# Gated linear attention and an MLP mixer on one core: block 5 by DMA transpose, batch 0 mixed into its transposed form, channel weights in three-chunk pieces, and another order

## The chip, the cores and the metric

One core of one Trainium2 chip runs the whole program in one launch. The metric is the device time in microseconds, a median of three runs. Inputs and the output lie in device memory as float32; matrix products run in bfloat16 with float32 sums in PSUM. The core has five instruction streams: PE (TensorE, matrix products), DVE (VectorE), ACT (ScalarE), POOL (GpSimd) and SP (SyncE, which here only issues transfers). The transfers themselves run on sixteen DMA engines that all queues share.

## The reference, cut to what matters

```python
B, H, S, D = 4, 8, 768, 48                      # batch, heads, time, head size
for t in range(S):                              # gated linear attention
    state = alpha[:, :, t, :, None] * state + k[:, :, t, :, None] * v[:, :, t, None, :]
    y[:, :, t] = einsum('bhd,bhde->bhe', q[:, :, t], state)
x = y as (B, S, H * D)                          # (4, 768, 384)
h  = relu(x.T @ w_tok1) @ w_tok2                # over time: 768 -> 256 -> 768
u  = x + h.T
h2 = relu(u @ w_ch1) @ w_ch2                    # over channels: 384 -> 1536 -> 384
out = u + h2
```

## The kernel before

**Blocks.** Time is cut into three blocks of 256 steps for each batch, so there are twelve attention blocks, 0 to 11 (block n belongs to batch n // 3). A block loads alpha, k, q and v (`ld_at`, `ld_kt`, `ld_qt`, `ld_vt`, 384 KB each, in runs of 384 bytes). Logarithms, a cumulative sum on PE (`cum`) and exponentials (`E`, `IE`) give the decay factors. Keys and queries are multiplied with them (`kk`, `qq`), transposed, multiplied with each other on PE (`G0`, `G1`), masked on DVE (`mask0`, `mask1`, a 128x1024 product each) and multiplied with v (`y0`, `y1`), together with what the carried state gives (`ia`, `ib`). `K`, `s`, `sa` and `sm` make the state. `x0` and `x1` take the two halves of the result out of PSUM. A block thus gives two of the six 128-row tiles x of its batch.

**How keys and queries are transposed.** In the blocks of KX and QX (6 to 11) by a DMA transpose that SP issues (`dk`, `dq`), and the query is then put in its final order by a copy (`pq`). In blocks 0 to 5 by eight PE transposes each (`trk`, `trq`) and a copy out of PSUM (`evk`, `evq`).

**Mixers.** For each batch: `t1` (12 products, 128x384) and `ht` (relu) give the hidden tokens, `t2` (12 products) and `u` (six adds of PSUM and x on DVE) give u with time on the partitions. u is then transposed into ut: in batch 0 (UP) on PE (`up`, 18 transposes of 128x128) with three copies `ut`; in batches 1 to 3 by two DMA transposes `ux_b_0`, `ux_b_1`, one for each half of u. `c1_b_mc_half` (three products; 24 of them in a batch) and `rt` (relu, ACT or DVE) give the hidden channels, `c2_b_i_q` (three products; 24 of them) and `o` (PSUM plus u, DVE) the output rows, which `st` stores.

**Weights.** Sixteen pieces of 384 KB (`ldw_`) are cast to bfloat16 by `cw_`. A piece of w_ch1 (`wc1`) is 128 of its 384 rows by 768 columns, so that a `c1` needs three pieces; a piece of w_tok2 (`wt2`) is 128 rows by 768 columns, and a `t2` needs both.

**What sets the order.** Nothing is scheduled at run time. The string ORDER names every operation with the engine that runs it (t PE, s ACT, v DVE, g POOL, y SP), and each engine does its operations in that order; BUFS gives the buffers. An operation at the head of its engine's list that waits holds up everything behind it there. `fN_` ahead of an operation are fillers: N products of 128x512 on zeros, which keep PE running (three of them are issued as one float32 product). SP's list holds all loads, all DMA transposes and some of the stores. Loads share 19 buffers of one class (`in`), so a load also waits until the former content of its buffer has been used.

Of the kernel before, what the change touches and what calls it, by code (L numbers as in the profile page):

```python
# [34 lines left out]
def dve(n, two=False):  # L35
    return {"DVE": (64 + n / (1.92 if two else 0.96), 157 + n / (1.92 if two else 0.96))}
# [61 lines left out]
KX = (6, 7, 8, 9, 10, 11)  # L98
QX = (6, 7, 8, 9, 10, 11)
KFN = 0  # L100
LAST = (3, 0)
UP = (0,)
# [18 lines left out]
def build(g):  # L121
# [8 lines left out]
    def fillers():  # L130
        for o in list(P.ops):
            nm = o.name
            if "PE" in o.eng and (nm[:4] in ("t1_0", "t2_0", "up_0") or nm.split("_")[-1][-1] in "0123" and nm[:2] not in ("t1", "t2", "up", "c1", "c2") and not nm.endswith("10") and not nm.endswith("11")):
# [182 lines left out]
    def mixer(b):  # L316
# [27 lines left out]
        uts = []
        if b in UP:
            for p in range(3):
                bank = V("one")
                o = P.op(f"up_{b}_{p}", pe([128] * 6), m0 + (3900 + 340 * p) * sc, writes=[bank],
                         reads=list(dict.fromkeys([us[2 * p][0], us[2 * p + 1][0]])),
                         preds=[us[2 * p][1], us[2 * p + 1][1]],  # L350
                         emit=lambda e, p=p, bank=bank: g.utr(bank, [us[2 * p][0], us[2 * p + 1][0]], p))
                uts.append(P.op(f"ut_{b}_{p}", either(dve(768, True), act(768)), m0 + (3950 + 340 * p) * sc, writes=[ut],
                                reads=[bank], preds=[o], emit=lambda e, p=p, bank=bank: g.utev(e, ut, bank, p)))
        else:
            for half in range(2):
                uts.append(P.op(f"ux_{b}_{half}", {"SP": (1240.0, 1240.0)}, m0 + (3900 + 500 * half) * sc, writes=[ut],
                                reads=[us[3 * half][0]], preds=[us[3 * half + i][1] for i in range(3)],
                                emit=lambda e, half=half: g.uxbar(ut, us[3 * half][0], half),
                                dma=("x", 1450.0, 1180.0, 480.0)))
        rts = []  # L360
        for mc in range(NDC):
            rt = V("rt")
            ro = []
            for half in range(2):
                bank = V("one")
                o = P.op(f"c1_{b}_{mc}_{half}", pe([384] * 3), m0 + (4900 + 975 * mc + 487 * half) * sc, writes=[bank],
                         reads=[ut], preds=(uts[0:2 + half] if b in UP else [uts[half]]) + [wl[("wc1", p)] for p in ((0, 1, 2) if mc < 6 else (3, 4, 5))],
# [5 lines left out]
        for i in range(NS):  # L373
            hold = 4000.0 if (i >= NS - 3 and b < B - 1) else 0.0
            cuts = [(0, HD // 2), (HD // 2, HD)] if (b, i) == LAST else [(0, HD)]
            for ci, (ca, cz) in enumerate(cuts):
# [3 lines left out]
                for q4 in range(4):  # L380
                    pp = []
                    for mc in range(3 * q4, 3 * q4 + 3):
# [6 lines left out]
                          reads=[bank, us[i][0]], preds=[prev],  # L389
# [576 lines left out]
```

## Time and profile before

| | us |
|---|---|
| median of 3 runs (162.3 to 162.38) | 162.38 |
| span of the profiled execution, first to last instruction | 160.5 |
| around the span, taking the profiled execution to have run like the median | 1.9 |
| PE busy | 154.6 |
| DVE, ACT, POOL busy | 114.9, 97.8, 80.8 |
| first product of mixer 0's `c1` | at 31.76 |
| first product of mixer 1's, 2's, 3's `c1` | at 67.80, 100.91, 133.81 |

The page of the profile has the busy time of each engine, then the span in 40 slices of 4.0 us with a digit (tenths) for each engine and for the DMA engines, and the groups of instructions by line of the source. The time line gives starts and durations, merged where one line runs several times in a row ("x12"). The DMA share of a stretch can come out above 1, so it is read against other stretches of the same trace. Times of a row are microseconds from the span's start; "mean ns" is the duration of one instruction. Matmuls follow each other faster than their duration, since they are pipelined.

### The profile page before, as it was taken

The page shows a single profiled execution, that of the slowest core. Times are in us where ns is not written, and L with a number is a line of the kernel's source. Part 1 is how long each engine was busy: PE and PEld are TensorE (multiplying, and loading weights), DVE is VectorE, ACT ScalarE, POOL GpSimd, SP SyncE. Part 2 cuts the span into 40 slices and gives each one's busy share as a digit, 9 for nine tenths or more (in the row PEclk, how much of TensorE's full clock was granted, in tenths as well). Part 3 has the DMA queues.
Part 4 walks back from the last instruction along what each step waited for, and adds up shares of the span by engine and source line. Part 5 has one row for each costly group of instructions (what it writes and reads, how often), then busy time and mean ns, then how long its engine had stood idle before and what let it go on. Part 6 is the DMA issues. An engine that isn't in the chain of part 4 may idle for free.

```text
span 160.5 us, 3971 instructions
## 1 busy us (share of the span) xinstructions
PE 154.6 (96%) x1563; PEld 97.1 (60%) x1563; DVE 114.9 (72%) x206; ACT 97.8 (61%) x179; POOL 80.8 (50%) x94
## 2 busy tenths in 40 slices
PE   7999989999999999999999999999999999999992
PEld 2545565766667676666667666566567665665661
DVE  6099994979889787989969758795886762464222
ACT  3789999998899955897563583269832203343000
POOL 5205897695973649389778852699523000000000
PEclk9999999999999999999999999999999999999999
DMA  4999999999999999999989999989701235111133
GB/s 122 320 324 317 317 374 311 339 333 306 316 347 324 275 278 272 210 228 319 241 202 298 239 315 204 217 196 134 196 21 62 87 79 169 49 49 53 49 129 116
DMA packets 76130, 35.05 MB, mean 218 GB/s; under 512 B 70352, under 2 KB 74320, under 8 KB 76112
## 3 DMA queue, kind: packets, MB, share of 16 engines
q1 hardware_dynamic: 73808, 31.76, 74.1%
q10 hardware_dynamic: 2304, 3.05, 5.3%
q8 instruction: 12, 0.20, 0.5%
q14 instruction: 6, 0.05, 0.1%
HBM read 25.17 MB, written 4.72 MB: 186 GB/s over the span
## 4 chain that ended last, share of the span: by engine, by line
PE 61%; DMA 12%; DVE 6%; ACT 6%; SPq 6%; POOL 4%; issue 3%; DVEq 0%; POOLq 0%
PE ps L907 22%; PE ps L902 21%; PE ps L643 11%; DMA in<-in_v_dram 6%; SPq L584 6%; DMA out_dram<-o 4%; PE ps L878 3%; PE ps L883 2%; DMA ut<-u 2%; DVE pkk L700 2%; DVE gtm L770 1%; PE ps L712 1%; DVE rt L875 1%; POOL vb L746 1%; POOL pkq L700 1%
## 5 line engine op out<-in xcount | busy, mean ns | idle before, releaser
L907 PE MATMUL ps<-wc,rt 128*128 128x384 bf16 (+1 forms) x300 | 52.4, 319 | 0.0
L902 PE MATMUL ps<-ut,wc 128*128 128x384 bf16 x288 | 50.3, 326 | 0.1
L902 PEld LDWEIGHTS <-wc 128*128 128x128 bf16 x288 | 27.1, 98 | 17.9 <-DMA ut<-u 0.6
L907 PEld LDWEIGHTS <-rt 128*128 128x128 bf16 x300 | 27.8, 98 | 16.0
L873 ACT ACTIVATE rt<-ps 128x384 bf16<-128x384 f32 x47 | 21.4, 492 | 23.6 <-PE ps L902 23.3
L875 DVE TENSOR_SCALAR rt<-ps 128x384 bf16<-128x384 f32 x49 | 25.6, 551 | 9.1 <-PE ps L902 8.9
L770 DVE TENSOR_TENSOR gtm<-ps,mk 128x1024 bf16<-128x1024 f32 x24 | 28.5, 1218 | 3.1 <-PE ps L643 2.8
L911 DVE TENSOR_TENSOR o<-ps,u 128x384 f32<-128x384 f32 (+1 forms) x25 | 13.2, 536 | 12.6 <-PE ps L907 10.1
L700 POOL TENSOR_TENSOR pkk<-in,IE 128x768 bf16<-128x768 f32 x8 | 14.5, 1817 | 3.3 <-DVE ss L844 2.3
L745 ACT CAST x<-ps 128x384 bf16<-128x384 f32 x20 | 9.2, 479 | 11.1 <-PE ps L643 9.5
L887 DVE TENSOR_TENSOR u<-ps,x 128x384 bf16<-128x384 f32 x24 | 12.0, 550 | 3.1 <-PE ps L883 2.5
L746 POOL CAST vb<-in 64x384 bf16<-64x384 f32 (+1 forms) x14 | 8.3, 594 | 10.4 <-DMA in<-in_v_dram 4.7
L692 POOL TENSOR_TENSOR in<-in,in 128x384 f32<-128x384 f32 x8 | 8.0, 1000 | 10.5 <-DVE u L887 3.8
L643 PE MATMUL ps<-rt 128*128 128x512 bf16 (+1 forms) x29 | 12.1, 515 | 1.1 <-DVE rt L541 1.1
L745 ACT CAST vb<-in 64x384 bf16<-64x384 f32 (+1 forms) x18 | 11.4, 634 | 0.8 <-DMA in<-in_v_dram 0.3
L700 POOL TENSOR_TENSOR pkq<-in,E 128x768 bf16<-128x768 f32 x6 | 10.9, 1818 | 0.6 <-DMA tpk<-pkq 0.3
L878 PE MATMUL ps<-x,wt 128*128 128x384 bf16 x48 | 11.0, 325 | 0.0
L844 POOL TENSOR_TENSOR ss<-tmp,E 128x384 bf16<-128x384 f32 x10 | 8.3, 833 | 4.2 <-DVE in L628 3.9
L841 DVE TENSOR_TENSOR tmp<-ps,ss 128x384 f32<-128x384 f32 x16 | 8.8, 552 | 1.8 <-PE ps L643 0.6
L883 PE MATMUL ps<-ht,wt 128*128 128x384 bf16 x48 | 9.1, 326 | 0.0
L643 PE MATMUL ps<-vb,gtm 128*128 128x48 bf16 x192 | 8.2, 183 | 0.2 <-DVE gtm L770 0.2
L643 PE MATMUL ps<-tpq,tpk 48*64 48x128 bf16 (+1 forms) x288 | 7.9, 218 | 0.4 <-POOL tpq L746 0.3
(94 smaller groups left out, 207.6 us busy)
## 6 DMA issues: line engine op xcount, KB each, us to landing
in<-in_alpha_dram SPq DMA_DIRECT2D x12, 384.0 KB, 5.1
in<-in_v_dram SPq DMA_DIRECT2D x12, 384.0 KB, 5.6
in<-in_k_dram SPq DMA_DIRECT2D x12, 384.0 KB, 5.2
in<-in_q_dram SPq DMA_DIRECT2D x12, 384.0 KB, 5.5
in<-in_moe_w_ch_dram SPq DMA_DIRECT2D x12, 384.0 KB, 5.9
out_dram<-o ACTq DMA_DIRECT2D x15, 192.0 KB, 1.8
in<-in_moe_w_tok_dram SPq DMA_DIRECT2D x4, 384.0 KB, 6.0
out_dram<-o SPq DMA_DIRECT2D x8, 192.0 KB, 2.2
```

The costliest lines, as they stand in the source:

```text
L643: return self.pe.matmul(out, lhsT=lhsT, rhs=rhs, start=start, stop=stop, skip_group_check=True)
L700: self.shared(self.eng[e].tensor_tensor(self.t(dst)[:, :, h0:h1, 0:D], self.t(src)[:, h0:h1].rearrange("p h s d -> p s h d"), bass.AP(tens ...
L745: return self.act.copy(d, s)
L770: self.nc.vector.tensor_tensor(self.t(gtm)[:, hf, :, :], self.pair(gp).rearrange("p a (j t) -> p (a j) t", t=128), bass.AP(tensor=m.tensor ...
L873: self.act.activation(d, s, AF.Relu)
L875: self.nc.vector.tensor_scalar_max(d, s, 0.0)
L878: self.pe.matmul(self.bank(bank)[:, 0:HD], lhsT=self.wt1[:, kc, m * 128 : m * 128 + 128], rhs=self.t(x), start=(kc == 0), stop=(kc == NS - 1))
L883: self.pe.matmul(self.bank(bank)[:, 0:HD], lhsT=self.wt2[:, kc, i * 128 : i * 128 + 128], rhs=self.t(hts[kc]), start=(kc == 0), stop=(kc = ...
L887: self.nc.vector.tensor_tensor(self.t(u)[:, i % 3], self.bank(bank)[:, 0:HD], self.t(x), ALU.add)
L902: self.pe.matmul(self.bank(bank)[:, 0:HD], lhsT=self.wc1[:, kc, mc * 128 : mc * 128 + 128], rhs=self.t(ut)[:, 3 * half : 3 * half + 3, kc, ...
L907: self.pe.matmul(self.bank(bank)[:, 0 : cz - ca], lhsT=self.t(rts[mc][0])[:, i * 128 : i * 128 + 128], rhs=self.wc2[:, mc, ca:cz], start=( ...
L911: self.nc.vector.tensor_tensor(self.t(o)[:, ca:cz], self.bank(bank)[:, 0 : cz - ca], self.t(u)[:, i % 3, ca:cz], ALU.add)
```

## The change

Four things, and then one list in place of another.

1. KX and QX begin with 5: block 5's `trk`, `trq`, `evk` and `evq` go, and `dk5`, `dq5` (DMA transposes issued by SP) and `pq5` (a copy, on POOL) come.
2. Batch 0 (UDIR) makes u directly in its transposed form. `xa_0_half_j` (three products of 128x128 with the identity) puts the transposed x into a PSUM bank, `tt_0_half_j` (two products of 128x384) adds the transposed token mix to it, and one copy `ut_0_half_j` takes the bank out as ut. The outputs still need u with time on the partitions, so two DMA transposes `un_0_0` and `un_0_1` make it from ut, and the adds `o_0_i` wait for them. `t2_0`, `u_0` and `up_0` are gone.
3. A piece of `wc1` is now 256 columns of all three row chunks (runs of 1 KB instead of 3 KB), and a `c1` needs one piece. A piece of `wt2` is 384 columns of both row chunks, and a `t2` or `tt` needs one.
4. ORDER and BUFS are other lists.

```diff
-KX = (6, 7, 8, 9, 10, 11)
-QX = (6, 7, 8, 9, 10, 11)
+KX = (5, 6, 7, 8, 9, 10, 11)
+QX = (5, 6, 7, 8, 9, 10, 11)
-UP = (0,)
+UP = ()
+UDIR = (0,)
...
+                    xa = P.op(f"xa_{b}_{half}_{j}", pe([128] * 3), ...
+                    o = P.op(f"tt_{b}_{half}_{j}", pe([384] * 2), ...
+                             reads=[h for h, _ in hts], preds=[h for _, h in hts] + [xa, wl[("wt2", half)]],
+                    evs.append(P.op(f"ut_{b}_{half}_{j}", either(act(384), dve(384)), ...
+                un = P.op(f"un_{b}_{half}", {"SP": (1240.0, 1240.0)}, m0 + 6000 * sc, writes=[u], reads=[ut], preds=evs,
...
-                         ... [wl[("wc1", p)] for p in ((0, 1, 2) if mc < 6 else (3, 4, 5))],
+                         ... [wl[("wc1", mc // 2)]],
...
-                          reads=[bank, us[i][0]], preds=[prev],
+                          reads=[bank, us[i][0]], preds=[prev, us[i][1]],
...
-            self.gated(dma(t, self.w[2][128 * c : 128 * c + 128, 768 * h : 768 * h + 768]), op)
+            self.gated(dma(t.rearrange("p (c m) -> p c m", c=3), w[:, :, 256 * piece : 256 * piece + 256]), op)
...
+    def xadd(self, bank, xs, j):
+        for i, x in enumerate(xs):
+            self.mm(self.bank(bank)[:, i * 128 : i * 128 + 128], self.t(x)[:, j * 128 : j * 128 + 128], self.idn, i == 0, False)
+
+    def tok2t(self, bank, half, j, hts):
+        for kc in range(NDT):
+            self.mm(self.bank(bank)[:, 0:HD], self.t(hts[kc])[:, j * 128 : j * 128 + 128],
+                    self.wt2[:, half, kc, :], False, kc == NDT - 1)
+
+    def utev3(self, e, ut, bank, half, j):
+        self.copy(e, self.t(ut)[:, 3 * half : 3 * half + 3, j, :], self.bank(bank)[:, 0:HD].rearrange("p (i t) -> p i t", i=3))
+
+    def unat(self, u, ut, half):
+        self.nc.sync.dma_start_transpose(self.t(u).rearrange("p i (j c) -> p (i j) c", j=NM),
+                                         self.t(ut)[:, 3 * half : 3 * half + 3].rearrange("p i j t -> p (i j t)"))
```

Parts of the lists that the prediction speaks of, sorted by engine from the two ORDER strings.

SP's list of before, up to the transposes of mixer 1's u:

```
at1 at0 vt0 kt0 qt0 kt1 vt1 at2 qt1 kt2 qt2 vt2 wt10 at3 wt11 wt21 wt20 at4 kt3 wc14 wc13 wc15 qt3 wc11 wc10 wc12 vt3
at5 qt4 kt4 wc21 wc20 wc22 kt5 wc23 qt5 vt4 wc24 wc25 at6 at7 vt5 kt7 at8 kt6 qt6 qt7 kt8 vt6 dk6 ux_1_0 st_0_0 dq6 ux_1_1
```

SP's list of after, up to the same point:

```
at0 at1 kt0 qt0 vt0 kt1 at2 qt1 vt1 kt2 qt2 at3 vt2 wt10 wt11 qt3 kt3 wt21 wt20 wc11 wc10 wc13 at4 wc14 vt3 wc12 qt4 wc15
at5 kt4 wc21 kt5 wc20 wc22 qt5 wc23 vt4 wc24 vt5 dk5 wc25 dq5 un_0_0 at6 at8 kt6 un_0_1 at7 kt8 qt6 vt6 qt7 ux_1_0 kt7 ux_1_1
```

Further parts of after's lists:

```
DVE: ... qq2 mask1_1 sa1_1 mask0_1 mask0_2 x1_1 sa0_2 mask1_2 q0r3 k0a3 qq3 ht_0_1 evq3 ut_0_1_1 ...
DVE: ... o_0_2 o_0_1 mask1_5 mask0_5 x1_5 k0a6 o_0_3 ht_1_0 u_1_1 u_1_2 u_1_0 u_1_4 o_0_4 u_1_3 u_1_5 ...
PE:  ... xa_0_1_0 xa_0_1_1 trq3 tt_0_1_0 xa_0_1_2 tt_0_1_2 tt_0_1_1 tt_0_0_1 trk3 tt_0_0_0 tt_0_0_2 c1_0_1_1 ...
PE:  ... c2_0_4_3 cum6 t2_1_1 t2_1_0 t2_1_2 t2_1_4 c2_0_0_3 t2_1_3 t2_1_5 c2_0_5_0 c2_0_5_1 c2_0_5_2 cum8 c2_0_5_3
     cum7 c1_1_1_0 ...
```

Fillers: 36 units in before (8+1, 8+1, 1, 1, 2, 4, 3, 2, 1, 1, 3), 24 in after (8+1, 2, 4+1, 3, 3, 2).

More of the change, by code (lines that the diff above doesn't have):

```diff
@@ L132, in fillers @@
             nm = o.name
-            if "PE" in o.eng and (nm[:4] in ("t1_0", "t2_0", "up_0") or nm.split("_")[-1][-1] in "0123" and nm[:2] not in ("t1", "t2", "up", "c1", "c2") and not nm.endswith("10") and not nm.endswith("11")):
+            if "PE" in o.eng and (nm[:4] in ("t1_0", "t2_0", "up_0", "xa_0", "tt_0") or nm.split("_")[-1][-1] in "0123" and nm[:2] not in ("t1", "t2", "up", "c1", "c2", "xa", "tt") and not nm.endswith("10") and not nm.endswith("11")):
                 bank = V("one")
@@ L366, in mixer @@
                 o = P.op(f"c1_{b}_{mc}_{half}", pe([384] * 3), m0 + (4900 + 975 * mc + 487 * half) * sc, writes=[bank],
-                         reads=[ut], preds=(uts[0:2 + half] if b in UP else [uts[half]]) + [wl[("wc1", p)] for p in ((0, 1, 2) if mc < 6 else (3, 4, 5))],
+                         reads=[ut], preds=(uts[half] if b in UDIR else uts[0:2 + half] if b in UP else [uts[half]]) + [wl[("wc1", mc // 2)]],
                          emit=lambda e, mc=mc, half=half, bank=bank: g.ch1(bank, ut, mc, half))
@@ L470 @@
[L470 to L474 removed]
+ld_at0y ln0s f8_cumw0t f1_cumw0t cumw0t ld_at1y ln1s IE0s ld_kt0y cumw1t kk0v ld_qt0y E0s qq0v f2_trk0t trk0t evk0v
```

219 lines of the change are left out of this document (120 added, 99 removed), and 22 rows, old and new, of the table BUFS.

## The prediction

> **What bounds the kernel now.** I read the page's busy lines and slices first, then the windows, the waits of PE's weight loads, and the time line around the places where one mixer follows another.
>
> ```profile
> PE 154.6 (96%) x1563; PEld 97.1 (60%) x1563; DVE 114.9 (72%) x206; ACT 97.8 (61%) x179; POOL 80.8 (50%) x94
> ...
> PE   7999989999999999999999999999999999999992
> ...
> DMA  4999999999999999999989999989701235111133
> ```
>
> ```profile
> 5.00:27.70 22.70, 21.45 (x267) 12.56 (x265) 17.31 (x22) 20.53 (x33) 13.45 (x16) 1.00 1.12 328
> 31.80:62.00 30.20, 30.10 (x329) 20.06 (x330) 25.73 (x41) 26.63 (x49) 20.20 (x23) 1.00 1.05 312
> 62.00:66.00 4.00, 4.00 (x26) 2.44 (x25) 3.24 (x7) 1.71 (x5) 2.93 (x4) 1.00 0.89 202
> 66.00:97.00 31.00, 31.00 (x359) 20.03 (x357) 25.90 (x46) 21.53 (x45) 23.47 (x22) 1.00 1.04 263
> 31.80:157.50 125.70, 125.15 (x1246) 80.40 (x1246) 91.25 (x154) 71.42 (x140) 62.38 (x64) 1.00 0.75 200
> 157.50:160.50 3.00, 0.00 (x0) 0.00 (x0) 0.30 (x1) 0.00 (x0) 0.00 (x0) 1.00 0.27 98
> ```
>
> A row has the stretch, its length, the busy time of PE, PEld, DVE, ACT and POOL, the clock, the DMA share and GB/s. From 31.8 to 157.5 PE is busy for 125.15 of 125.70 us at full clock: there only less work on PE can save time. Ahead of that it is busy with fillers too. But the DMA engines are as full: their share is 1.12 when nothing holds them up (5 to 27.7), and 1.05, 0.89 and 1.04 up to 97. So two resources are nearly full, and they meet where a mixer's first `c1` waits for the transposed u:
>
> ```profile
> PEld L902 <- DMA ut<-u: 0.6, 2, 0.5
> ```
>
> ```profile
> 59.29 1.61 SPq L584 DMA_DIRECT2D in<-in_v_dram  x1
> 62.89 1.33 SPq L725 DMA_TRANSPOSE tpk<-pkk  x1
> 64.68 1.29 SPq L729 DMA_TRANSPOSE ut<-u  x1
> ...
> in<-in_v_dram SPq DMA_DIRECT2D x1, 384.0 KB, 5.8
> ...
> tpk<-pkk SPq DMA_TRANSPOSE x1, 3.4
> ...
> ut<-u SPq DMA_TRANSPOSE x1, 2.9
> ```
>
> ```profile
> 31.76 4.55 PE L902 MATMUL ps<-ut,wc 128*128 128x384 bf16 x27
> ...
> 67.80 2.60 PE L902 MATMUL ps<-ut,wc 128*128 128x384 bf16 x15
> ...
> 100.91 3.82 PE L902 MATMUL ps<-ut,wc 128*128 128x384 bf16 x21
> ```
>
> The last number of a transfer's row is the time from issue to landing. The 49th load (`ld_vt6`) lands at 59.29 + 5.8 = 65.1, `dk6` at 66.3, `ux_1_0` at 64.68 + 2.9 = 67.6, and mixer 1's `c1` starts at 67.80. The PE list is met by the DMA train with 0.2 us to spare; that point decides.
>
> **The change, part by part.**
>
> *Start, up to mixer 0's `c1`.* The second block's q is the 11th transfer in both lists, and DVE's list hangs on it.
>
> ```profile
> 11.88 1.14 SPq L584 DMA_DIRECT2D in<-in_q_dram  x1
> ...
> in<-in_q_dram SPq DMA_DIRECT2D x1, 384.0 KB, 6.2
> ...
> 19.03 2.36 DVE L770 TENSOR_TENSOR gtm<-ps,mk 128x1024 bf16<-128x1024 f32 x2
> ...
> L700 DVE TENSOR_TENSOR pkq<-in,E 128x768 bf16<-128x768 f32 x6 | 5.7, 955 | 0.3 <-POOL in L628 0.2
> L887 DVE TENSOR_TENSOR u<-ps,x 128x384 bf16<-128x384 f32 x24 | 12.0, 550 | 3.1 <-PE ps L883 2.5 <-issue 0.4
> 27.73 2.28 PE L883 MATMUL ps<-ht,wt 128*128 128x384 bf16 x12
> ...
> 30.52 0.33 PE L643 MATMUL ps<-la,u 128*128 128x384 bf16 x1
> ...
> 30.81 0.61 PE L712 MATMUL ps<-idn,pkk 128*128 128x128 bf16 x8
> ...
> 36.14 0.61 PE L712 MATMUL ps<-idn,pkq 128*128 128x128 bf16 x8
> 36.59 2.60 PE L902 MATMUL ps<-ut,wc 128*128 128x384 bf16 x15
> ```
>
> It lands at 11.88 + 6.2 = 18.1. From there DVE has, up to `ht_0_1`, two products of 768 (0.96 each), four masks (2.36 / 2 = 1.18), and five operations of 384 (0.55): 1.9 + 4.7 + 2.75 = 9.4, or some 9.0 since each starts a little before the one ahead of it ends. `ht_0_1` runs from 27.1 to 27.7. Then PE has twelve `tt` products (2.1 by the row of `t2`), three of an `xa` (0.2) and `trk3` (eight transposes, 36.59 - 36.14 = 0.45): 2.7. `c1` starts at about 30.4, 1.4 us sooner than 31.76, with 12 filler units fewer. `trq3` is then done (0.45) and `cum4` is not (30.81 - 30.52 = 0.3), worth another 0.2.
>
> *Block 5.* Two times eight PE transposes go, at 0.45 each: 0.9 us off PE. The products `G0_5`, `G1_5` become twice as many of half the size; that is even:
>
> ```profile
> 55.80 0.62 PE L643 MATMUL ps<-tpq,tpk 48*128 48x128 bf16 x16
> ...
> 73.11 0.64 PE L643 MATMUL ps<-tpq,tpk 48*64 48x128 bf16 x32
> L746 POOL COPY tpq<-tpk 128x1024 bf16<-128x1024 bf16 x4 | 5.3, 1335 | 1.9 <-PE ps L902 1.8
> ```
>
> `pq5` costs POOL 1.3 us, off the path. SP gets two transposes.
>
> *u of batch 0.* 18 products of 128 columns stand for 18 transposes of 128, and `tt` for `t2`: even on PE. DVE loses six adds (3.3 us). SP gets two more transposes. What waits for them: `o_0_2` stands ahead of block 5's masks on DVE, and `o_0_3`, which needs `un_0_1`, stands ahead of `ht_1_0` and of mixer 1's `u` adds.
>
> *Weight pieces.* No `c1` of before waited for weights, so one piece in place of three is worth nothing alone. Its runs of 1 KB lie between the 384 bytes of the inputs and the 3 KB of the pieces before, and all kinds together average 1.27 us a transfer (worked out below); I count nothing for the DMA, and 0.1 for each of six pieces as the dear end.
>
> *The DMA train.* Ahead of `ux_1_0` there were 49 loads and `dk6`; now there are 48 loads and `dk5`, `dq5`, `un_0_0`, `un_0_1`. A load takes (65.1 - 4.2) / 48 = 1.27 us of the train, with the first at 0.81 + 3.4 = 4.2:
>
> ```profile
> in<-in_alpha_dram SPq DMA_DIRECT2D x1, 384.0 KB, 3.4
> ...
> tpk<-pkq SPq DMA_TRANSPOSE x1, 5.9
> ```
>
> A transpose takes SP 1.3 us and follows the one ahead by as much (66.3, 67.6); the dearest one of the trace, among loads at 104, needed 5.9 to land. The Trainium skill, "DMA: Bandwidth & Descriptors", section "Latency and other measured facts", gives transposes an effective 261 GB/s; for 256 KB and 288 KB that is an estimate of 1.0 and 1.1 us, 4.3 instead of 5.2 for four, and the sum would end 0.9 us lower. The row is 1.3, and the measurement decides.
>
> So `ux_1_0` can land at 65.1 - 1.3 (a load fewer) - 0.6 (a store of half the size that ran there before) + 4 x 1.3 + 1.3 (its own) = 69.7, if before had no room. It had: 30.2 x (1 - 1.05 / 1.12) = 1.9 us. The bounds are 67.8 and 69.7.
>
> *The PE and DVE lists at that point.* From `c1` to `c1`, before needed 67.80 - 31.76 = 36.0; after has one `cum` more (0.3) and three `trk`, `trq` fewer (1.35): 35.0, thus 65.4. It also waits for the last piece of `wc2`, which was the 39th transfer and is the 41st behind a load and a transpose:
>
> ```profile
> in<-in_moe_w_ch_dram SPq DMA_DIRECT2D x1, 384.0 KB, 4.3
> 44.09 2.35 SPq L607 DMA_DIRECT2D in<-in_moe_w_ch_dram  x2
> L745 ACT CAST wc<-in 128x768 bf16<-128x768 f32 x9 | 7.5, 857 | 0.1
> ```
>
> It was issued at about 46.0 and landed at 50.3, now 52.9 to 53.9, cast at 53.7 to 54.7. Up to `c2_0_2_3`, PE has 36 groups of three at 0.49 (the 27 from 31.76 to 36.14) and some 4.6 us for blocks 3 and 4, so it is there by 30.4 + 17.6 + 4.6 = 52.6. That is 1 to 2 us of waiting: 66.9 by PE's list. By DVE's: `un_0_1` is the 47th transfer, 4.2 + 42 x 1.27 + 4 x 1.3 = 62.7, less up to 1.9; then `o_0_3` and `ht_1_0` (0.55 each), three `t2` (1.0), the last `u` (1.0) and `ux_1_0` (2.9): 66.8 to 68.7.
>
> I take 69.0 for mixer 1's `c1`, nearer to the DMA's later bound because its transposes now lie between loads: **1.2 us later than 67.80**. The 2.5 us won on PE are spent, and more.
>
> *To mixer 2's `c1`.* The PE list is 100.91 - 67.80 = 33.1, less one `cum`: 32.8, thus 101.8. The train was also just in time there (the second of the two waits above). It owes 5.2 us; it has 1.9, and 4 x (1 - 0.89 / 1.12) + 31 x (1 - 1.04 / 1.12) = 0.8 + 2.2. So it comes 0.3 to 5.2 later than 100.9; I take 102.3, that is 0.5 past the PE list. Behind that the DMA is light and PE's list is the same but for the `cum` (0.3): 160.5 - 100.9 + 0.3 = 59.9, with a tail of 3.0 as before.
>
> **Sum:** 102.3 + 59.9 = 162.2 us of span, 1.7 more than 160.5. With 1.9 around it: 164.1 us (profile and median of before are 160.5 and 162.38).
>
> **Rivals.**
>
> 1. *The train takes the transposes in its idle room.* Then the start's 1.6 and block 5's 0.9 us are kept, but for the wait on weights: `c1` of mixer 1 at 65.4 to 66.9, and the span 158.1 to 159.6: 160.0 to 161.5 us. For it speak the 0.89 at 62 to 66; against it that `ux_1_0` must land before 67.5, below the lower bound. It turns there: each of the four must cost under 1.2 us and all 1.9 us of room be used. Chance 0.30.
> 2. *Transposes among loads cost two to three times as much,* as at 104 (5.9 to land). One to two more of 1.3 us for two to four of them put mixer 1's `c1` at 71 to 73; with 32.8 and 59.9 behind it the span is 164 to 166: about 167 us. Chance 0.12.
> 3. *Both sides meet:* the start's 1.6 and block 5's 0.9 pay for the wait, 162.4 us. Chance 0.07.
>
> **How the numbers follow.** A measurement of this kernel can tell 0.2% (0.3 us) from no change. The forecast's own range is 162.8 to 166, chance 0.51. Faster 0.30, the same 0.07, slower 0.51 + 0.12 = 0.63. The range leaves out the lower part of rival 1 and the upper of rival 2: 160.3 to 166.8.
>
> **What would show it.** Right: `c1` of mixer 0 near 30.4; waits of PE's weight load or of DVE's `o` on a DMA between 50 and 70; `ux_1_0` landing after 67.8; a DMA share over 1.05 from 31.8 to 69; `c1` of mixer 1 after 68.5. Wrong: `c1` of mixer 1 before 67.5, or a `c1` of mixer 0 later than 31.5, which would put the loss at the start.

## The result, and the profile after

The changed kernel takes **171.16 us** (median of 4 runs, 169.53 to 171.79), the kernel before 162.38 beside it: 1.050 times as long, with a 95% interval of 1.043 to 1.057. The forecast was 164.1 with a range up to 166.8: the sign was right, the size was not. (Ratios below are to the kernel before on the same chip and leave disturbed executions out, so that they can differ a little from the quotient of two medians.)

The page of after, the lines that answer to those of before, and its busiest DMA queue (packets, MB, the time of its packets as a share of sixteen engines' span):

```profile
PE 155.5 (91%) x1553; PEld 96.3 (57%) x1553; DVE 113.0 (66%) x200; ACT 95.5 (56%) x180; POOL 82.9 (49%) x95
...
PE   7798899999998959999996799899699999999992
...
PEclk9999999999999996999999879999999999999999
DMA  4999999999999999999999993999261005401033
...
q1 hardware_dynamic: 80512, 33.56, 78.4%
```

The windows of after, in the stretches that were shown of before (length, busy time of PE, PEld, DVE, ACT and POOL, clock, DMA share, GB/s):

```profile
31.80:62.00 30.20, 29.71 (x310) 18.51 (x309) 24.49 (x39) 22.95 (x44) 18.86 (x21) 1.00 1.10 283
62.00:66.00 4.00, 1.91 (x11) 1.05 (x10) 2.30 (x5) 1.48 (x4) 1.63 (x2) 0.93 1.03 276
66.00:97.00 31.00, 28.14 (x301) 17.40 (x300) 20.64 (x35) 16.37 (x32) 24.71 (x24) 0.94 1.17 262
```

PE is busy for about as long as before (155.5 against 154.6 us), some of it at a lower clock; the span is longer mainly because PE now has holes. Before, it was busy for 4.00 of 4.00 us at 62 to 66 and for all of 66 to 97; now for 1.91 and 28.14, and the clock is below 1. The DMA share has gone up in the same stretch, from 0.89 and 1.04 to 1.03 and 1.17.

PE's time line has the starts of `c1` (ps<-ut,wc) and the long waits (in brackets: idle before, and what ended it):

```profile
30.59 0.66 PE L944 MATMUL ps<-ut,wc 128*128 128x384 bf16 x3
...
64.11 1.48 PE L909 MATMUL ps<-ht,wt 128*128 128x384 bf16 x8 [2.09 <-DVE ht L901]
...
71.00 9.91 PE L944 MATMUL ps<-ut,wc 128*128 128x384 bf16 x60
...
94.65 0.64 PE L669 MATMUL ps<-tpq,tpk 48*64 48x128 bf16 x32 [2.55 <-DMA tpk<-pkk]
...
109.09 5.54 PE L944 MATMUL ps<-ut,wc 128*128 128x384 bf16 x33 [0.46 <-DMA ut<-u]
...
123.44 0.64 PE L669 MATMUL ps<-tpq,tpk 48*64 48x128 bf16 x32 [1.48 <-ACT tpq L771]
```

| stretch | before | forecast | after |
|---|---|---|---|
| up to mixer 0's `c1` | 31.76 | 30.4 | 30.59 |
| to mixer 1's `c1` | 36.04 | 38.6 | 40.41 |
| to mixer 2's `c1` | 33.11 | 33.3 | 38.09 |
| to the end | 59.6 | 59.9 | 61.0 |

The third row of the table has the largest difference to the forecast. Its window in after and in before:

```profile
71.00:109.09 38.09, 34.88 (x365) 21.87 (x364) 24.87 (x43) 22.38 (x45) 26.93 (x27) 0.96 1.05 237
```

```profile
67.80:100.91 33.11, 33.11 (x372) 21.26 (x370) 27.40 (x47) 20.64 (x43) 23.62 (x22) 1.00 1.04 255
```

Of the 5.0 us more, PE is idle for 3.2, of which 2.55 are the wait for `dk8`. The other 1.8 are time in which it is busy for longer: behind that wait the clock is 0.50 for 3.4 us (96.13 to 99.54), and half of that is 1.7.

Behind the waits stand transposes. SP's and DVE's time line, and the landing times (last number, us from issue) of `un_0_1`, `ux_1_0` and `dk8`:

```profile
56.23 3.03 SPq L939 DMA_TRANSPOSE u<-ut  x1
...
66.33 2.28 SPq L755 DMA_TRANSPOSE ut<-u  x1
...
88.29 2.51 SPq L751 DMA_TRANSPOSE tpk<-pkk  x1
...
63.03 0.56 DVE L953 TENSOR_TENSOR o<-ps,u 128x384 f32<-128x384 f32 x1 [2.00 <-DMA u<-ut]
...
u<-ut SPq DMA_TRANSPOSE x1, 6.8
...
ut<-u SPq DMA_TRANSPOSE x1, 4.6
...
tpk<-pkk SPq DMA_TRANSPOSE x1, 6.3
```

Before, SP mostly took 1.3 us for a transpose (1.9 for three of eighteen) and it landed after 2.7 to 3.8, but for two (4.4 and 5.9). Now most of those from 46 to 95 us take SP 1.8 to 3.0 us and land after 3.7 to 6.8. `o_0_3` waits for `un_0_1` (2.00), `ht_1_0` stands behind it on DVE, and PE behind that (2.09).

### The profile page after: what moved, and what is told of

Read it like the earlier page. It is cut to its first block, busy times and chain, and to the rows that moved or that the text cites. A ratio compares the mean times of both kernels' runs of the same rounds, so it can differ in the third digit from the quotient of the medians.

```text
span 170.1 us, 3956 instructions
## 1 busy us (share of the span) xinstructions
PE 155.5 (91%) x1553; PEld 96.3 (57%) x1553; DVE 113.0 (66%) x200; ACT 95.5 (56%) x180; POOL 82.9 (49%) x95
## 3 DMA queue, kind: packets, MB, share of 16 engines
q1 hardware_dynamic: 80512, 33.56, 78.4%
## 4 chain that ended last, share of the span: by engine, by line
PE 54%; DMA 20%; DVE 8%; POOL 8%; SPq 3%; issue 3%; ACT 2%; POOLq 0%; DVEq 0%
PE ps L944 25%; PE ps L949 18%; PE ps L669 7%; DMA ut<-u 5%; DMA u<-ut 4%; DMA tpk<-pkk 4%; DMA tpk<-pkq 4%; POOL pkk L726 3%; DVE gtm L796 3%; DMA in<-in_alpha_dram 3%; PE ps L904 2%; DVE pkq L726 2%; DMA out_dram<-o 2%; SPq L608 2%; POOL vb L772 1%
## 5 line engine op out<-in xcount | busy, mean ns | idle before, releaser
L949 PE MATMUL ps<-wc,rt 128*128 128x384 bf16 (+1 forms) x300 | 56.2, 328 | 0.3 <-ACT wc L771 0.3
L899 ACT ACTIVATE rt<-ps 128x384 bf16<-128x384 f32 x51 | 23.8, 492 | 22.8 <-PE ps L944 22.7
L901 DVE TENSOR_SCALAR rt<-ps 128x384 bf16<-128x384 f32 x45 | 23.5, 552 | 12.5 <-PE ps L944 12.3
L726 POOL TENSOR_TENSOR pkq<-in,E 128x768 bf16<-128x768 f32 x8 | 14.5, 1816 | 1.8 <-DVE in L722 1.4
L654 POOL TENSOR_TENSOR in<-in 128x384 f32<-128x384 f32 x9 | 8.9, 996 | 9.0 <-DMA in<-in_alpha_dram 5.4
L771 ACT CAST x<-ps 128x384 bf16<-128x384 f32 x16 | 7.3, 480 | 9.3 <-PE ps L669 9.2
L913 DVE TENSOR_TENSOR u<-ps,x 128x384 bf16<-128x384 f32 x18 | 9.1, 550 | 5.0 <-PE ps L909 4.9
L772 POOL CAST vb<-in 64x384 bf16<-64x384 f32 (+1 forms) x18 | 10.6, 591 | 0.7
L669 PEld LDWEIGHTS <-tpk 48*64 48x64 bf16 (+1 forms) x304 | 5.9, 103 | 8.1 <-issue 4.2
L669 PE MATMUL ps<-rt 128*64 128x384 f32 (+1 forms) x19 | 8.0, 527 | 1.1 <-DVE rt L565 1.1
```

The source lines that it names most:

```text
L669: return self.pe.matmul(out, lhsT=lhsT, rhs=rhs, start=start, stop=stop, skip_group_check=True)
L726: self.shared(self.eng[e].tensor_tensor(self.t(dst)[:, :, h0:h1, 0:D], self.t(src)[:, h0:h1].rearrange("p h s d -> p s h d"), bass.AP(tens ...
L771: return self.act.copy(d, s)
L772: return self.shared(self.eng[e].tensor_copy(d, s))
L899: self.act.activation(d, s, AF.Relu)
L901: self.nc.vector.tensor_scalar_max(d, s, 0.0)
```

## The experiments

Four theories were open. **T**: the four new transposes each cost more of the DMA train than the 1.3 us that were counted. **D**: it is DVE's wait at `o_0_3`. **C**: it is the lower clock behind PE's waits. **O**: it is the new order itself. The runs have short names: those that begin with a are after with one thing undone, those with b are before with one thing done.

### One cause at a time

*DVE's wait* (a1). `o_0_3` goes behind mixer 1's adds.

```diff
-DVE: ... x1_5 k0a6 o_0_3 ht_1_0 u_1_1 u_1_2 u_1_0 u_1_4 o_0_4 u_1_3 u_1_5 ...
+DVE: ... x1_5 k0a6 ht_1_0 u_1_1 u_1_2 u_1_0 u_1_4 o_0_4 u_1_3 u_1_5 o_0_3 ...
```

> The kernel after, with the add o_0_3 and its store moved on DVE's list from ahead of ht_1_0 to behind the last u add of mixer 1 (u_1_5); all four new transposes keep their places. Theory T (the transposes among loads hold the DMA train up): ux_1_0 is issued as soon as u is there, but the train is as full as before; c1 of mixer 1 starts at 69.5 to 71.0 instead of 71.0, and the time stays within 1 us of 171. Rival D (it is DVE's wait for un_0_1 ahead of mixer 1's adds that costs, with the low clock behind it): the PE wait of 2.1 us at 62 to 64 and the clock of 0.5 at 66 to 68 go, c1 of mixer 1 starts at 67.5, and the time is about 167.

Measured: 170.68 us, 1.038 (1.029 to 1.047). PE's wait for `ht` is gone, and a longer one stands at `c1`:

```profile
72.39 12.85 PE L944 MATMUL ps<-ut,wc 128*128 128x384 bf16 x60 [4.88 <-DMA ut<-u]
```

D falls: mixer 1's `c1` hangs on its own transpose `ux_1_0`, whatever DVE does. `ux_1_0` is now issued at 65.39 instead of 66.33, but the last load ahead of it (`ld_qt7`) lands at 71.2, in after at 69.9, and `ux_1_0` 1.1 us behind that load in both. What is left of a gain, some 2 us, is within the two intervals.

*The clock* (a10). PE is kept busy in the two long waits.

```diff
+    for nm, z in (("t2_1_1", 9), ("G0_8", 11)):      # z products of 128x512 on a constant, ahead of nm
```

> The kernel after with PE kept busy in its two long waits: nine products of 512 columns (1.9 us) on a constant, into a bank of their own, ahead of t2_1_1 and eleven (2.3 us) ahead of the products G of half 0 of block 8. No wait for data is taken away. Theory C (the granted clock falls because PE is idle for over 2 us there): the clock stays at 1.0 from 60 to 100 us, and the time is 3 to 3.5 us under that of after, 168 to 168.5. Rival N (the clock falls for another reason, or the time hangs on DMA alone there): 171 to 172, with the clock down again or with the waits as much longer.

Measured: 171.13 us, 1.049 (1.046 to 1.053), as after.

```profile
60.00:70.00 10.00, 9.88 (x91) 6.02 (x88) 4.98 (x11) 3.74 (x9) 5.97 (x5) 1.00 1.18 280
70.00:100.00 30.00, 27.46 (x312) 17.06 (x312) 20.65 (x34) 17.13 (x33) 21.18 (x23) 1.00 1.15 252
...
72.34 9.91 PE L953 MATMUL ps<-ut,wc 128*128 128x384 bf16 x60 [2.46 <-DMA ut<-u]
```

The clock is 1.00 throughout (after has 0.83 at 60 to 70), and the time is the same: PE gets to `c1` sooner and waits there for `ux_1_0`. From mixer 0's to mixer 1's `c1` it takes 40.42 us, in after 40.41: there the clock falls in time in which PE would have had to wait anyway. From mixer 1's to mixer 2's `c1` this profile has 36.39 instead of 38.09, so there the clock may cost up to 1.7 us; the medians, 171.13 and 171.16, show no gain. C falls as the main cause, and a part of the second stretch stays open.

*The two transposes back* (a2). `un_0_0` and `un_0_1` go, and the `o` of batch 0 read the transposed tile as it lies; the kernel leaves out the turning back.

```diff
-                un = P.op(f"un_{b}_{half}", {"SP": (1240.0, 1240.0)}, ...
-                us += [(u, un)] * 3
+                us += [(ut, evs[-1])] * 3
```

> The kernel after without the transposes of u of batch 0 back to tokens (un_0_0, un_0_1): the o adds of batch 0 read the transposed tile as it lies, so the turning back is left out of the computation. Two of the four new transposes fewer. Theory T: they took 6.8 and 3.7 us to land and kept the loads behind them; c1 of mixer 1 starts at 66.5 to 67.5 and, with dq5 and dk5 still there, the time is 165 to 167. Rival D (only the wait of DVE for un_0_1 costs): the same as with o_0_3 moved alone, about 167. Rival O (the new order of the instructions costs, not the transposes): 170 to 171.

Measured: 168.57 us, 1.035 (1.028 to 1.042).

```profile
68.71 3.55 PE L940 MATMUL ps<-ut,wc 128*128 128x384 bf16 x20 [0.96 <-DMA ut<-u]
...
q1 hardware_dynamic: 78144, 32.97, 77.0%
```

Mixer 1's `c1` comes 2.3 us sooner, and the median is 2.6 lower. That is T for two of the transposes, and about half of what T expected.

*Block 5 back on PE* (a3).

```diff
-KX = (5, 6, 7, 8, 9, 10, 11)
-QX = (5, 6, 7, 8, 9, 10, 11)
+KX = (6, 7, 8, 9, 10, 11)
+QX = (6, 7, 8, 9, 10, 11)
```

> The kernel after with keys and queries of block 5 transposed on PE again (trk5, evk5 on ACT, trq5, evq5 on ACT at the places of dk5, dq5, pq5); un_0_0 and un_0_1 stay. PE gets 0.9 us of work back. Theory T: dk5 and dq5 held the train for 3 to 5 us, un_0_1 lands that much sooner, c1 of mixer 1 at 67.5 to 69, and the time is 166 to 168. Rival D (only the un transposes with what waits for them cost): 171 to 172. Rival O (the order): 171 to 172.

Measured: 171.36 us, 1.052 (1.044 to 1.060).

```profile
57.11 0.56 PE L949 MATMUL ps<-wc,rt 128*128 128x384 bf16 x2 [1.88 <-ACT wc L771]
...
q1 hardware_dynamic: 78400, 33.04, 75.3%
```

The queue's packets take 127.1 us (75.3% of 168.8) instead of 133.4, and no time is won, where T expected 166 to 168: the two evictions were put on ACT ahead of the cast of `wc2`'s last piece, and PE now waits 1.88 us for that.

*None of the four* (a4), both edits at once:

> The kernel after with block 5 on PE and without the transposes of u of batch 0 back to tokens (left out of the computation): none of the four new transposes, but the new order, the weight pieces, and u made transposed in PSUM. Theory T: the train is that of the kernel before; c1 of mixer 0 at 30.5, of mixer 1 at 66 to 66.8, of mixer 2 at 99 to 100; the time is 159 to 161, below the kernel before. Rival O (the new order or the pieces cost by themselves): 165 or more.

Measured: 171.33 us, 1.050 (1.043 to 1.056), where T expected 159 to 161. This is the run that T did not foresee.

```profile
95.68 0.64 PE L665 MATMUL ps<-tpq,tpk 48*64 48x128 bf16 x32 [2.04 <-DMA tpk<-pkk]
...
q1 hardware_dynamic: 76032, 32.45, 72.5%
```

The late cast is in it as well (1.87), so it was run again (a12) with `evk5` on DVE and `evq5` on ACT behind that cast:

> None of the four new transposes (the turning back of u of batch 0 is left out of the computation, block 5 on PE), as in the earlier run of this kind, but the two evictions of block 5 no longer stand ahead of the cast of the last piece of wc2 on ACT: evk5 is on DVE, evq5 on ACT behind that cast. Theory: that run's wait of 1.9 us for the cast goes, ux_1_0 is no longer held up, and c1 of mixer 1 comes 35.5 to 37 us behind c1 of mixer 0 instead of 39.0 (after: 40.4); the stretch to mixer 2 stays at 37 to 38.5 by the new order; the time is 166 to 168.5. Rival (the order of the first stretch costs too): 39 us again, 170 or more.

Measured: 171.11 us (168.9 to 171.6), 1.047 (1.041 to 1.054). The profile is of the run of 168.9. From mixer 0's to mixer 1's `c1` it takes 38.76 us, where 35.5 to 37 were expected, and from there to mixer 2's 36.92. Windows, SP, one landing and one wait of it, with before's window of the same stretch as the last line:

```profile
60.00:70.00 10.00, 8.96 (x88) 5.83 (x87) 6.97 (x14) 5.61 (x13) 6.91 (x7) 1.00 0.46 126
70.00:100.00 30.00, 27.04 (x323) 17.21 (x322) 20.36 (x33) 17.50 (x35) 21.49 (x22) 1.00 1.15 256
...
55.98 1.14 SPq L604 DMA_DIRECT2D in<-in_q_dram  x1
65.22 1.35 SPq L751 DMA_TRANSPOSE ut<-u  x1
...
tpk<-pkk SPq DMA_TRANSPOSE x1, 6.3
...
93.26 0.64 PE L665 MATMUL ps<-tpq,tpk 48*64 48x128 bf16 x32 [2.00 <-DMA tpk<-pkk]
```

```profile
60.00:70.00 10.00, 10.00 (x81) 6.23 (x80) 8.28 (x16) 7.55 (x17) 7.01 (x7) 1.00 1.01 253
```

With the train light, SP has issued all that stands ahead of `ux_1_0` by 57.1 and then stops for 8 us, because `ux_1_0` needs u, and u comes at 65. The loads behind it on SP's list wait too: the DMA share is 0.46 at 60 to 70 (before 1.01). Then ten loads and the transposes come at once, one among the other; the share is 1.15, `dk8` lands after 6.3 us, and PE waits 2.00 for it. So the order loses there by itself a large part of what the transposes no longer take: mixer 1's `c1` is at 69.15, against 71.00 in after and 67.80 before. In after the same place is filled by the late train, and SP waits only 0.7 us.

### The pieces and u in the order of before

The pieces alone (b1):

> The kernel before with the new pieces of the weights alone (wt2 by halves of its columns, wc1 by 256 columns of all three chunks), in the order of before. Theory M: no difference, 162.0 to 162.8. Rival W (the pieces' runs of 1 KB are dearer for the transfers): the loads up to 30 us come later by 0.1 to 0.3 us for each of eight pieces, and the time is 163 to 164.

```diff
-KX = (5, ...); UP = (); UDIR = (0,); ORDER, BUFS of after
+KX = (6, ...); UP = (0,); UDIR = (); ORDER, BUFS of before
```

Measured: 162.81 us, 1.001 (0.997 to 1.005): the pieces cost nothing. With them, u of batch 0 made transposed (b3):

> The kernel before with the new pieces and with u of batch 0 made transposed in PSUM, in the order of before: the products of x with the identity stand ahead of where the first t2 stood, and un_0_0, un_0_1 stand together on SP behind the last piece of wc2. Block 5 stays on PE. Theory M: c1 of mixer 0 starts about 1 us sooner (30.5 to 31); the two transposes stand behind loads, the second lands behind the first in 4 to 5 us, and they push ld_at6 and those behind it back by 3 us; o_0_0 and o_0_5 wait little; the time is 161 to 163. Theory T (each of the transposes costs the full train 2 us or more): c1 of mixer 1 at 70 or later, 165 to 167.

```diff
-PE: ... f3_t2_0_0 t2_0_0 ... up_0_0 up_0_1 ... up_0_2 ...       SP: ... wc25 at6 ...
+PE: ... xa_0_0_0 ... xa_0_1_2 tt_0_0_0 ... tt_0_1_2 ...         SP: ... wc25 un_0_0 un_0_1 at6 ...
```

Measured: 165.15 us, 1.010 (1.004 to 1.017). The busiest queue of the kernel with the pieces alone, and of this one; and mixer 0's `c1`:

```profile
q1 hardware_dynamic: 75600, 31.76, 73.6%
```

```profile
q1 hardware_dynamic: 77968, 32.35, 76.4%
...
31.48 4.56 PE L944 MATMUL ps<-ut,wc 128*128 128x384 bf16 x27 [0.79 <-POOL wc L772]
```

73.6% of 161.0 is 118.5 us, 76.4% of 162.9 is 124.5: the queue's packets took 6.0 us longer with the two transposes. Mixer 1's `c1` is at 69.76 and the time 165.15, which is nearer to theory T (70 or later, 165 to 167) than to M (161 to 163). `c1` could have started 0.8 sooner; the cast of the one piece that it needs was late on POOL.

### Loads among transposes

In before, `dk8`, `dq7`, `dk7` and `dq8` stand in one row. Two loads are moved between them (b4):

```diff
-SP: ... at9 vt7 qt8 at10 dk8 dq7 dk7 st_0_2 dq8 vt8 at11 ...
+SP: ... at9 vt7 qt8 dk8 at10 dq7 vt8 dk7 st_0_2 dq8 at11 ...
```

> The kernel before with three loads moved in between the transposes dk8, dq7, dk7, dq8, which stand in one row there: ld_at10 from ahead of dk8 to behind it, ld_vt8 from behind dq8 to behind dq7, ld_at11 stays behind dq8. Nothing else is moved. Theory M: dq7, dk7 and dq8 take 4.5 to 6 us to land instead of 3.3, 2.9 and 2.7, SP takes 2 us or more for each, PE waits for G of block 7 or 8 on them, and the time is 164 to 166. Rival P: each lands within 4 us, and the time is within 0.5 us of before.

Measured: 166.52 us, 1.019 (1.010 to 1.027).

```profile
77.72 1.52 SPq L725 DMA_TRANSPOSE tpk<-pkq  x1
...
80.27 2.03 SPq L725 DMA_TRANSPOSE tpk<-pkk  x1
...
tpk<-pkq SPq DMA_TRANSPOSE x1, 4.8
...
tpk<-pkk SPq DMA_TRANSPOSE x1, 4.3
...
85.30 0.34 PE L643 MATMUL ps<-vb,pkk 128*128 128x96 bf16 x4 [2.61 <-POOL pkk L746]
```

`dq7` and `dk7` land after 4.8 and 4.3 us instead of 3.3 and 2.9, and `dk7` is issued 2.0 later. POOL's copy `kc7` waits for it, and PE waits 2.61 us for the copy. From mixer 1's to mixer 2's `c1` it takes 36.19 instead of 33.11: two loads in the wrong place cost 3.1 us. `dq8`, which was expected to be late as well, lands after 3.0.

### The same thing turned round in after

The reverse was tried in after's list: its transposes in rows. First, all six from `dq6` to `dk8`, with the loads ahead and behind (a5):

> The kernel after, with SP's list alone regrouped between 70 and 93 us: the three loads ahead of and between dq6, dk6, dq7, dk7 (ld_at9, ld_vt8, ld_vt7) go ahead of dq6, and the three between dk7, dq8, dk8 (ld_at11, ld_vt10, ld_at10) behind dk8; so the six transposes stand in one row. Theory M (a transpose issued right behind loads takes 5 to 6 us to land, one behind another transpose 3 to 4): dk8 lands in 3 to 4 us instead of 6.3, PE's wait of 2.6 us at 94 and the low clock behind it go, the stretch from c1 of mixer 1 to c1 of mixer 2 is 34 to 35 us instead of 38.1, and the time is 167 to 168. Rival P (the producers on POOL and DVE set when the transposes are issued; where they stand does not matter): the stretch stays at 37 to 38 and the time at 171.

Measured: 172.38 us, 1.055 (1.049 to 1.062). `dk8` lands after 2.7 us, but the stretch still takes 37.77: `ld_vt7` had to wait 1.3 us for its buffer there, with everything behind it, and `dk8` then waited for `kk8`. So, with another buffer, and `kk8` sooner on POOL (a6):

```diff
-SP: ... dq6 dk6 at9 vt8 dq7 vt7 dk7 at11 dq8 vt10 at10 dk8 qt9 ...    POOL: ... qq8 pq7 vb8 kk8 ...
+SP: ... dq6 dk6 at9 vt8 vt7 dq7 dk7 dq8 dk8 at11 vt10 at10 qt9 ...    POOL: ... qq8 kk8 pq7 vb8 ...
```

> The kernel after, with the transposes dq7, dk7, dq8, dk8 in one row on SP: ld_vt7 (with another buffer, so that SP does not wait for it) goes ahead of dq7, the loads ld_at11, ld_vt10, ld_at10 behind dk8, and on POOL the product kk8, which dk8 waits for, goes ahead of pq7 and vb8. Theory M (what costs is the loads among the transposes): dk7, dq8 and dk8 land in 2.7 to 4 us instead of 5.2, 4.9 and 6.3; dk8 is there by 88 instead of 94.6; PE's wait of 2.6 us at 94 and the low clock behind it go; from c1 of mixer 1 to c1 of mixer 2 it takes 34 to 35.5 us instead of 38.1, and the time is 168 to 169. Rival P (something else takes the place of that wait): the stretch stays over 37 us and the time at 171.

Measured: 173.79 us, 1.069 (1.064 to 1.073).

```profile
86.63 1.26 SPq L751 DMA_TRANSPOSE tpk<-pkk  x1
...
tpk<-pkk SPq DMA_TRANSPOSE x1, 2.9
...
93.78 0.99 POOL L654 TENSOR_TENSOR in<-in 128x384 f32<-128x384 f32 x1 [1.20 <-DMA in<-in_alpha_dram]
...
96.21 0.41 PE L669 MATMUL ps<-tpq,tpk 48*64 48x128 bf16 x15 [1.94 <-DVE tmp L867]
```

`dk8` lands after 2.9 us, at 89.5 instead of 94.6, as expected. But the load `at11`, now behind it, holds up POOL (`P11`), which holds up DVE and PE: the stretch takes 38.27. Two more kernels with this row, one with `un_0_1` right behind `un_0_0` (a7), one with `qt11` ahead of `dq9` besides (a8):

> The same, and un_0_1 moved on SP from behind ld_at6, ld_at8, ld_kt6 to right behind un_0_0, so that dq5, un_0_0 and un_0_1 stand in one row. Theory M: un_0_1 lands at 57 to 58 instead of 63, o_0_3 no longer holds up ht_1_0, PE's wait of 2.1 us at 62 to 64 and the low clock behind it go; c1 of mixer 1 at 67.5 to 69 instead of 71; the time is 164.5 to 166.5. Rival P: the loads of blocks 6 and 8, now 2 to 3 us later, take the place of the wait: c1 of mixer 1 at 70 or later, and the time is that of the row alone.

> The same as the one with the row and un_0_1, and ld_qt11 moved ahead of dq9, behind ld_vt11, so that no load is under way when dq10 is issued. Theory M: dq10 lands in 3 to 4 us instead of 6.1, PE's wait of 1.5 us at 123 goes, and the time is 1 to 2 us under that of the kernel without this move. Rival P: dq9 lands later by 1 us or more, G of block 9 waits, and the time is the same within 0.5 us.

Measured: 173.87 us for a7 (170.81 to 174.14, no interval), and 173.29, 1.060 (1.053 to 1.067) for a8. In both `un_0_1` lands after 3.0 us, and PE no longer waits long for `ht` (0.47 and 0.50). But the loads `qt6`, `vt6`, `qt7` stand ahead of `ux_1_0` as in after, which lands after 6.0: `c1` of mixer 1 at 72.01 and 71.36. In a8 the moved load `qt11` has landed at 111.25, and `dq10`, issued at 116.19 with no load under way, still takes 5.4 us to land, where 3 to 4 were expected. So a load is not the only thing that makes a transpose late; what it is here is not shown (ACT issues two stores, at 115.83 and 116.99). Then `P11` goes behind on POOL, with the four transposes and without (block 5 and the turning back as above); and `vb10` too:

```diff
-POOL: ... sm1_6 P9 P11 sm0_7 vb10 sm1_7 kc8 P10 ...
+POOL: ... sm1_6 P9 sm0_7 vb10 sm1_7 kc8 P11 P10 ...      (a11, a13)
+POOL: ... sm1_6 P9 sm0_7 sm1_7 kc8 vb10 P11 P10 ...      (a15, a16)
```

> The kernel with the row of dq7, dk7, dq8, dk8 (all four new transposes are in it), with the product P11 moved on POOL from ahead of the states of blocks 7 and 8 to just ahead of P10, so that POOL no longer waits for the load ld_at11, which the row had put off. Theory M (the loads among the transposes cost, and in the row's first form this wait on POOL took their place): c1 of mixer 1 to c1 of mixer 2 in 34.5 to 36 us instead of 38.1 to 38.3; the time is 168.5 to 170. Rival P (the stretch is bound by what the DMA engines have to move in it, however it is ordered): 37.5 us or more and 171 to 173.

> The same as that, with the row of dq7, dk7, dq8, dk8 and P11 ahead of P10. If the mixing of loads and transposes is what the new order costs from mixer 1 to mixer 2, this stretch takes 33 to 35 us, the first 35.5 to 37, and the time is 161.5 to 165, near the kernel before. If the stretch stays at 37 or more, the mixing isn't the cause: 166 to 168.

> The kernel with the row of dq7, dk7, dq8, dk8 and P11 ahead of P10 (all four new transposes are in it), and on POOL the cast vb10 moved from ahead of the states of block 7 to ahead of P11, so that POOL waits neither for ld_at11 nor for ld_vt10 in that stretch. Theory M (mixing): PE's waits of 1 us or more between 72 and 105 go; c1 of mixer 1 to c1 of mixer 2 in 34 to 36 us instead of 37.7 to 38.3; the time is 167.5 to 170. Rival P (a third wait comes up; the stretch is bound by how much the DMA engines move there): 37 us or more.

> The same without the four new transposes (the turning back of u of batch 0 left out, block 5 on PE with the evictions that don't stand ahead of the cast of wc2). Theory M: POOL's wait of 3.6 us for ld_vt10 and PE's of 3.3 us behind it go; the stretch takes 34 to 36 us instead of 40.2 and 36.9; the time is 164 to 167. Rival P: 37 us or more, and 168 or more.

| | us | ratio | mixer 1's to mixer 2's `c1` |
|---|---|---|---|
| a11, four transposes, `P11` behind | 174.56 | 1.057 (1.049 to 1.065) | 37.73 |
| a13, none of them, `P11` behind | 171.61 | 1.053 (1.047 to 1.059) | 40.20 |
| a15, four transposes, `vb10` too | 174.12 | 1.069 (1.060 to 1.078) | 37.41 |
| a16, none of them, `vb10` too | 171.72 | 1.054 (1.048 to 1.061) | 38.79 |

Rival P held each time. By a13's own expectation, a stretch of 37 or more means that the mixing of loads and transposes is not what the new order costs there. The wait that takes the place of the last one, in a13 (PE), and in a15 (POOL, then PE):

```profile
97.76 0.34 PE L665 MATMUL ps<-vb,pkk 128*128 128x96 bf16 x4 [3.27 <-POOL pkk L768]
```

```profile
103.47 1.00 POOL L718 TENSOR_TENSOR in<-in,in 128x384 f32<-128x384 f32 x1 [3.53 <-DMA in<-in_k_dram]
...
109.66 5.58 PE L944 MATMUL ps<-ut,wc 128*128 128x384 bf16 x33 [2.09 <-ACT E L702]
```

In a13 POOL waits 3.56 us for `vt10`; in a15 that is mended, and it waits 3.5 us for a key load further on. In these kernels, whatever went ahead in this stretch, something behind it came later. That would fit a stretch that is bound by what the queue must bring there, but no run shows that bound by itself.

*A whole version without the four* (a14). u of batch 0 is added in PSUM by three products of the transposed tile with the identity for each `o`, with the row and `P11` behind:

```diff
+        if ut is not None and q4 == 0:
+            for j in range(NM):
+                self.mm(self.bank(bank)[:, j * 128 : j * 128 + 128], self.t(ut)[:, i, j, :], self.idn, j == 0, False)
```

> A whole version without the four transposes: as that, but u of batch 0 is added to c2's sums by three products of the transposed tile with the identity into each o's bank (18 products of 128 columns, 1.0 us of PE in all), so that nothing has to be turned back; the o of batch 0 are copies on DVE. Expected 1 us behind the one that leaves the turning back out: 162.5 to 166 if the row helps, 167 to 169 if not. It beats the kernel before only if the first stretch takes under 36.5 us and the second under 33.5.

Measured: 173.52 us, 1.065 (1.059 to 1.072), with 38.74 and 37.77 us for the two stretches. No version that was run beats the kernel before; the pieces alone equal it.

## Why the prediction was wrong

**The start: right in this trace, too good as a rule.** 30.4 was forecast, 30.59 measured. But the fifteen other profiles of kernels with this start have 30.4 to 32.2, with after 31.3 on average, against 31.7 for the three profiles with before's start (before, b1, b4). The usual gain is 0.4 us, not 1.4, so the close agreement is in part luck.

**The weight pieces: right**, nothing (1.001). The wait for the last piece of `wc2` came as forecast, but at 0.32 us was shorter than the 1 to 2.

**The size of a transpose: the first step that failed.** The sum has 4 x 1.3 us, SP's time for a transpose in a row of its own kind. For one alone that is right: `ux_3_0` of after, with nothing beside it (144.4 to 145.7), has 1184 packets in 1.3 us. Among loads it is not. Behind `ldw_wc24` the same ten loads follow in all kernels with the new order, up to `ld_qt7`, the last one ahead of `ux_1_0`. In after `ldw_wc24` lands at 49.5 and `ld_qt7` at 69.9, 20.4 us later; in a12, without the four transposes, at 49.05 and 61.0, 11.9 later. Nine profiles with the four have 20.1 to 21.6, five without them 11.9 to 13.6. On average that is 7.7 us for four, 1.9 each, not 5.2 and 1.3.

The time of the busiest queue's packets grows too: 78.4% of 170.1, 133.4 us, with all four, and 123.1 without any (a4, 72.5% of 169.8). But it is no price of one transpose. The same transfers took 129.3 in a8 (76.2% of 169.7), and since the share of a stretch can come out above 1, packet time is not the train's time. Rival 2 had this mechanism, with a chance of 0.12; its 71 to 73 for mixer 1's `c1` came true (71.00), its 167 for the whole did not. The Trainium skill, "DMA: Bandwidth & Descriptors", section "Latency and other measured facts", gives transposes 261 GB/s, an estimate of 1.0 to 1.1 us. The trace has 1.3 for one alone and 1.9 among loads, and the measurement decides.

**The train's room: not shown either way.** It was read from a DMA share of 1.05 or 0.89 against a full 1.12, but after shows 1.17 where it is full of loads and transposes, so 1.12 was no ceiling. For the last load ahead of `ux_1_0` the forecast's terms without the four transposes give 61.3 with the room of 1.9 and 63.2 without it; the five profiles without them have 61.0 to 64.6.

**Mixer 1's `c1`: right in the issue, short in the landing.** `un_0_1` landed at 63.0 (62.7 less up to 1.9 was forecast), and `ux_1_0` was issued at 66.33, where 69.0 less 2.9 gives 66.1. It then took 4.6 us instead of 2.9, since the last load ahead of it landed only at 69.9: that 1.7 is most of the gap from 69.0 to 71.0. It is the train, by the term above, and not DVE's list (a1).

**To mixer 2's `c1`: the second step that failed, and the largest error, 4.8 of the 7.9 us of span.** 33.3 was forecast, from PE's work and a train 0.5 us late; 38.09 measured. That PE's list is the same there was true and said nothing. The forecast gave the new SP list no cost but that of the four transposes. Without any of them the stretch still takes 36.9 (a12) and 37.3 (a4), so at least 3.6 of the 4.8 belong to the new order. In after PE waits 2.55 us for `dk8`, which SP issues behind loads, and then has half the clock for 3.4 us. In before, two loads among transposes cost 3.1 us (b4). But in after's list the stretch did not get short when the loads were taken out from between the transposes (37.4 to 40.2), so what in the new order makes it long stays open.

**The end:** 59.9 forecast, 61.0 measured; `dq10` lands after 6.1 us, and PE waits 1.48 for its copy. Before, it took 5.9 and PE did not wait for it. The forecast said that DMA is light there, which is true and did not help this transpose; nor did taking the load away from it (a8, 5.4 us, a wait of 0.81).

**The precision.** The forecast took 0.2% as what a measurement can tell, from three runs of before that agree within 0.08 us. The interval of the result is 1.043 to 1.057, and effects under 1% can't be read from most of these runs.

So the 5.0% come apart like this. Leaving out the two transposes back is worth 1.5 points in the order of after (1.050 to 1.035); with block 5 on PE as well it is worth nothing that can be told (a3 1.052, a4 1.050, a12 1.047). In the order of before, making u transposed as a whole costs 1.0 (1.010 against 1.001). The pieces are worth nothing. With two of the four transposes out 3.5 points stay, with all four out 4.7 to 5.0: the new order, with the pieces and u made transposed still in it, costs about as much as the whole change. Block 5's part can't be told apart: without its DMA transposes its evictions need room on ACT and DVE that this order doesn't have, and the time is the same. That loads among transposes cost is shown by b4, in the order of before; that they are what the new list costs is not: every row that was tried in after ran into another wait, and the new list was not tried with before's SP list as a whole.

## What to carry to other kernels

Price a DMA transpose by how much later the loads behind it land, and by how late it lands itself among loads, not by its issue time in a row of its own kind: here 1.9 against 1.3 us. A change that brings another list needs a term for the list: here a kernel with the list and none of the four transposes took as long as the whole change. On a queue that issues in order, an operation that must wait for data (a transpose of something just computed) holds up every load behind it, so what stands behind it matters as much as what stands ahead. In an order that was made with the transposes in it, taking them out afterwards gave little back here; that a search with the right costs would do better was not tried.

## What was not expected of the hardware

In the profiles of before and after a transpose of 256 to 288 KB lands 2.7 to 3.7 us after its issue when no load is under way then, and 2.9 to 6.8 us when loads are; SP's time for issuing it goes from 1.23 to as much as 3.03. With no load under way it can still be late: 5.4 us for `dq10` in a8.

The clock fell behind some of PE's waits and not behind others as long. Windows of after, behind the wait of 2.09 us, and of b4, behind that of 2.61:

```profile
66.00:68.00 2.00, 2.00 (x8) 0.93 (x7) 1.08 (x3) 0.34 (x1) 1.96 (x2) 0.50 1.15 343
```

```profile
87.00:89.00 2.00, 2.00 (x39) 1.26 (x28) 1.55 (x2) 0.00 (x0) 2.00 (x3) 1.00 1.17 323
```

It is 0.50 in the one and 1.00 in the other. The Trainium skill, "TensorE: Matmul & The Clock Gate", section "Part 1: The HAM clock gate (the 'warmup' mystery)", puts half clock behind at least one idle window of about 3.4 us. The half agrees; the length does not, since 2.09 us were enough here, and 2.61 not always. Each time it stays low for 3.4 us (in after from 65.41 to 68.82 and from 96.13 to 99.54). Holding the clock up left the median where it was (171.13 against 171.16 us).
